# Crossbar transposes issued earlier on the sync queue, first V and pair copies on VectorE, smaller memsets, in a fused attention and maxout-FFN kernel

## The chip, the cores and the metric

The kernel runs on one core of a Trainium2 chip. The metric is device time in microseconds (us) of one execution; a profiled execution gives the trace, whose span is about 1.8 us shorter than that run's time. The granted clock is the share of TensorE's full clock that the profile shows it was given. On one core, a run over 1.5% above the fastest of its kernel is called slow, and ratios leave it out.

## The reference

The input is q, k and v of shape (8 batches, 12 heads, 448 positions, 64), and four 768x768 weights. In float32:

```
scores = q @ k^T / 8
m = max(scores);  e = exp(scores - m)
attn = e / (sum(e) + exp(-m) + 1e-9)          # softmax with one extra "off" slot
x = (attn @ v), heads side by side            # (3584, 768)
h = max(x @ w1, x @ w2, x @ w3)
out = h @ w_out                               # (3584, 768)
```

## The kernel before

Work is cut into 24 groups: 4 heads of one batch each, 3 groups to a batch. A group needs k and q transposed (head dimension on partitions) for the scores, V copied into a buffer with an added column (so that AV also gives the row sums), and its result x transposed again for the FFN. The FFN of a batch is cut into pieces of six matmuls (`p_i` up, `op_ps` out). TensorE's program interleaves the pieces with the scores and AV of later groups, so that it has work while ScalarE does the exponentials.

The first three groups (one batch) run in six half-groups, with k and q transposed by TensorE, as they still are for groups 3 and 4. From group 5 on, the crossbar of the DMA transposes them, issued on the sync queue:

```python
    def pair_qk(i):                       # two heads side by side, fp16; two buffers for each
        qf, kf = raw[i].pop("q"), raw[i].pop("k")
        ...
                nc.gpsimd.tensor_copy(out=t16, in_=f[:, 2 * pr : 2 * pr + 2].rearrange("p h c d -> p c h d"))

    def transpose_dma(i):                 # four crossbar transposes for a group
        ...
                nc.sync.dma_start_transpose(out=t[:, n * S : (n + 1) * S]..., in_=paired[i][pr][n]...)

    def prep_v(i):
        nc.gpsimd.tensor_copy(out=v_buf[i % NE][0:SC, :, :, 0:D], in_=raw[i].pop("v"))

    def x_transpose_dma(i):               # one crossbar transpose: x of a group, after AV and its division
        nc.sync.dma_start_transpose(out=xt_tile(b)..., in_=xn[i]...)
```

Stores of `out` go on the sync queue too; loads are issued by GpSimd. The loop over groups 3 to 23:

```python
    for i in range(3, NI):
        if i + 3 < NI:
            load_group(i + 3)
        if i + 2 < NI:
            pair_qk(i + 2)
        if i > 3:
            prep_v(i)
        ...
        for vi, units in enumerate(visits):           # three visits
            scores(i, units)
            # ... (i == 3 apart) fill with FFN pieces, which issue stores
                if vi < 2:
                    av(i - 1, vi)
                if vi == 1:
                    x_transpose_dma(i - 1)
                    if i + 1 < NI and i + 1 >= PE_QK:   # PE_QK = 5
                        transpose_dma(i + 1)
                fill(per / 6)
```

The waits that the framework adds are all on data and buffers. In the traces each engine's queue, the sync queue too, issues in program order.

The softmax here doesn't subtract the row's maximum and nothing guards it: scores larger than these inputs give would overflow.

Of the kernel before, what the change touches and what calls it, by code (L numbers as in the profile page):

```python
# [2 lines left out]

# [7 lines left out]
FP32 = mybir.dt.float32  # L11
# [10 lines left out]
def kernel(  # L22
# [11 lines left out]
    nc = tc.nc  # L34

    B, H, S, D = q.shape
# [3 lines left out]
    NCH = S // SC  # L40
    NDC = DM // 128
    NFC = DFF // 128
    GH = 4
    NG = H // GH
    NI = B * NG
    HQ = S // 2
# [4 lines left out]
    PE_QK = 5  # L51
# [32 lines left out]
    def load_group(i, which="qkv", step=GH):  # L84
        b, g = groups[i]
        tiles = raw.setdefault(i, {})
        for name in which:
            tiles[name] = ld_pool.tile(
                [SC, GH, NCH, D], MMDT, tag="ld_" + name, name="ld_" + name
            )  # L90
        for h0 in range(0, GH, step):
            for name in which:
                src = {"q": q, "k": k, "v": v}[name][b].rearrange(
                    "(g h) (p c) d -> g p h (c d)", g=NG, c=NCH
                )[g]
                nc.gpsimd.dma_start(  # L96
                    out=tiles[name][:, h0 : h0 + step].rearrange("p h c d -> p h (c d)"),
                    in_=src[:, h0 : h0 + step],
                )
# [22 lines left out]
    EW = NCH * S  # L122
    e_buf = [cpool.tile([128, GH * EW + 16], MMDT, name=f"e{j}") for j in range(NE)]
    v_buf = [cpool.tile([128, GH, NCH, D1], MMDT, name=f"vx{j}") for j in range(NE)]

    def e4(j):
        return e_buf[j][:, 0 : GH * EW].rearrange("p (h c s) -> p h c s", h=GH, c=NCH)

    for j in range(NE):
        nc.vector.memset(v_buf[j][:, :, :, D : D + 2], 1.0 / LAMBDA)  # L130
        nc.vector.memset(v_buf[j][96:128, :, :, 0:D], 0.0)
        nc.vector.memset(e4(j)[:, :, :, HQ : HQ + 16], 0.0)
        nc.vector.memset(e4(j)[96:128, :, 0, :], 1.0)
        nc.vector.memset(e4(j)[96:128, :, 1, 0:16], 0.0)
        nc.vector.memset(e_buf[j][:, GH * EW : GH * EW + 16], 0.0)

    def warm(n, cols=512):
        ps = ps_b.tile([128, 512], FP32, tag="b", name="warm")
# [5 lines left out]
    paired = {}  # L144
    qkT = {}

    def pair_qk(i):
        qf, kf = raw[i].pop("q"), raw[i].pop("k")
        got = []
        for pr in range(GH // 2):  # L150
            t = []
            for nm, f in (("k", kf), ("q", qf)):
                t16 = p16_pool.tile([SC, NCH, 2, D], MMDT, tag=f"{nm}16_{pr}", name=f"{nm}16_{pr}")
                nc.gpsimd.tensor_copy(  # L154
                    out=t16, in_=f[:, 2 * pr : 2 * pr + 2].rearrange("p h c d -> p c h d")
                )
                t.append(t16)
            got.append(t)
        paired[i] = got

    def transpose_pe(i, pr):

        trT = ps_b.tile([128, 2, S], MMDT, tag="b", name="trT")
        for n, nm in enumerate(("k", "q")):
            for c in range(NCH):
                if i in paired:
                    nc.tensor.transpose(
                        out=trT[:, n, ts(c, SC)], in_=paired[i][pr][n][:, c, :, :],
                        identity=ident16[0:SC, 0:SC],
                    )  # L170
                    continue
                for hh in range(2):
                    nc.tensor.transpose(  # L173
                        out=trT[hh * D : hh * D + D, n, ts(c, SC)],
                        in_=raw[i][nm][:, 2 * pr + hh, c, :],
                        identity=ident16[0:SC, 0:SC],
                    )
        t = att_pool.tile([2 * D, 2 * S], MMDT, tag="qkT", name="qkT")
        nc.vector.tensor_copy(out=t, in_=trT.rearrange("p n s -> p (n s)"))  # L179
        qkT[i, pr] = t  # L180

    def transpose_dma(i):
        for pr in range(GH // 2):
            t = att_pool.tile([2 * D, 2 * S], MMDT, tag="qkT", name="qkT")
            for n in range(2):
                nc.sync.dma_start_transpose(  # L186
                    out=t[:, n * S : (n + 1) * S].rearrange("p (c r) -> p c r", c=NCH),
                    in_=paired[i][pr][n].rearrange("p c h d -> p (c h d)"),
                )
            qkT[i, pr] = t  # L190
        paired.pop(i)

    def prep_v(i):
        nc.gpsimd.tensor_copy(  # L194
            out=v_buf[i % NE][0:SC, :, :, 0:D], in_=raw[i].pop("v")
        )

# [63 lines left out]
    def x_transpose_pe(i, qcs):  # L261
        b, g = groups[i]
        nq = len(qcs)
        tp = ps_b.tile([128, 2, nq, SC], MMDT, tag="b", name="xtp")
        for pr in range(2):
            for j, qc in enumerate(qcs):
                nc.tensor.transpose(
                    out=tp[:, pr, j, :],
                    in_=xn[i][:, pr, qc].rearrange("p h d -> p (h d)"),
                    identity=ident16[0:SC, 0:SC],  # L270
                )
        dst = xt_tile(b)[:, 2 * g : 2 * g + 2, qcs[0] * SC : (qcs[0] + nq) * SC]
        nc.vector.tensor_copy(out=dst, in_=tp.rearrange("p a j s -> p a (j s)"))
# [90 lines left out]
    def fill(cols):  # L364
        credit[0] += cols
        while pieces and credit[0] > 0:
            f, a, w = pieces.pop(0)
            f(*a)
            credit[0] -= w
        if not pieces:  # L370
            credit[0] = min(credit[0], 0.0)
# [13 lines left out]
    def half_scores(g, half, n):  # L385
        scores(g, half_units[n : n + 1], half * HQ, HQ)
# [6 lines left out]
    for n, (half, g) in enumerate(halves):  # L393
        for u in range(4):
            half_scores(g, half, u)
            if half == 0 and u in (0, 2) and tpose:
                transpose_pe(*tpose.pop(0))
            if half == 0 and u == 1:
                prep_v(g)
            if n > 0:  # L400
                ph, pg = halves[n - 1]
                if u == 0:
                    av(pg, 0, qh[ph])
                elif u == 2:
                    av(pg, 1, qh[ph])
                elif u == 3:
                    x_transpose_pe(pg, qh[ph])
                    if pg == NG - 1:
                        add_up(0, 0, HQ, [(i, f) for i in range(2) for f in (0, 2, 4)])
            fill(1.2 * UP if half == 1 else 0)  # L410
        if n == 1:
            load_weight(2)
            load_group(3, "v")
            load_group(4)
            load_weight(3)
        if n == 3:
            pair_qk(3)
        if n == 5:
            load_group(5)
            pair_qk(4)  # L420
            transpose_pe(3, 0)
            transpose_pe(3, 1)
            prep_v(3)


    visits = (((0, (0,)), (0, (1,)), (0, (2,))), ((0, (3,)), (1, (0,)), (1, (1,))), ((1, (2,)), (1, (3,))))
    for i in range(3, NI):
        b, g = groups[i]
        if i + 3 < NI:
            load_group(i + 3)  # L430
        if i + 2 < NI:
            pair_qk(i + 2)
        if i > 3:
            prep_v(i)
        if i >= 7 and i % 3 == 1:
            add_batch(i // 3 - 1)
        per = 0.0

        def share():
            nxt = 7 if i < 7 else (i - 1) // 3 * 3 + 4  # L440
            return left() / max(1, nxt - i)

        for vi, units in enumerate(visits):
            scores(i, units)
            if i == 3:
                halfq = qh[1]
                if vi == 0:
                    av(2, 0, halfq)
                    fill(UP)
                    av(2, 1, halfq)  # L450
                    x_transpose_pe(2, halfq)
                    add_up(0, HQ, HQ, [(w, f) for w in range(2) for f in (0, 2, 4)])
                    add_up(0, 0, HQ, [(2, f) for f in (0, 2, 4)])
                    add_up(0, HQ, HQ, [(2, f) for f in (0, 2, 4)])
                    add_out(0)
                    per = share()
                else:
                    if vi == 1:
                        transpose_pe(4, 0)
                        transpose_pe(4, 1)  # L460
                fill(per / 3)
            else:
                if vi == 0:
                    per = share()
                fill(per / 6)
                if vi < 2:
                    av(i - 1, vi)
                if vi == 1:
                    x_transpose_dma(i - 1)
                    if i + 1 < NI and i + 1 >= PE_QK:  # L470
                        transpose_dma(i + 1)
                fill(per / 6)

    av(NI - 1, 0)
    av(NI - 1, 1)
# [34 lines left out]
```

## Time and profile before

| | before |
|---|---|
| median of the first 3 runs | 425.34 us (419.53 to 425.52) |
| span of the profiled run | 421.8 us |
| TensorE busy | 355.0 us |
| mean granted clock | 0.949 |

The page's busy line, and two rows of its picture in 40 slices (busy tenths of TensorE, and its granted clock):

```profile
PE 355.0 (84%) x3438; PEld 203.7 (48%) x3438; DVE 181.5 (43%) x343; ACT 165.0 (39%) x193; POOL 133.4 (32%) x200
PE   5664989676799989799979969879968898899995
PEclk9995999896899999899989998998998999999999
```

TensorE is the engine to feed: it is idle for 67 us of the span, and no other engine is busy for half of the span. What TensorE's matmuls waited for (us in total, times, longest):

```profile
PE stp L207 <- DMA qkT<-q: 38.8, 19, 5.3
PE avp L237 <- POOL vx L194: 11.9, 2, 8.7
PE stp L207 <- DVE qkT L179: 4.9, 3, 4.4
PE avp L237 <- ACT e L216: 2.0, 3, 0.7
```

The first line is one wait for each of groups 5 to 23: the scores stand until the crossbar has brought the transposed q. Why it is late can be seen in one iteration. First the sync queue (`SPq`; start, length, what), then TensorE:

```profile
244.82 1.46 SPq L277 DMA_TRANSPOSE xT<-xn  x1
246.38 1.29 SPq L186 DMA_TRANSPOSE qkT<-k  x1
247.76 1.21 SPq L186 DMA_TRANSPOSE qkT<-q  x1
249.08 2.21 SPq L186 DMA_TRANSPOSE qkT<-k  x1
...
252.68 4.18 SPq L339 DMA_DIRECT2D out_dram<-o_sb  x6
```

```profile
242.61 1.21 PE L237 MATMUL avp<-vx,e 113*128 113x65 f16 x32
...
246.19 3.10 PE L316 MATMUL op_ps<-w,hT 128*128 128x384 f16 x18
253.15 1.30 PE L207 MATMUL stp<-qkT 64*128 64x448 f16 x6 [3.86 <-DMA qkT<-q]
```

x's transpose starts at 244.8, as soon as VectorE's division after the AV at 242.6 is done (244.79). Only then do those of k and q follow. TensorE ran out of other work at 249.3. The six score matmuls after this wait took 1.30 us; after waits of 1.6 us or less they take 0.74. After the long waits the granted clock is lower: it is 0.50 over the three microseconds from 253.15, and 1.00 again from 257.15.

In the start, AV of groups 0 and 2 waited for V copies in GpSimd's queue. TensorE, then GpSimd:

```profile
19.93 1.04 PE L237 MATMUL avp<-vx,e 113*128 113x65 f16 x16 [3.19 <-POOL vx L194]
...
37.62 1.04 PE L237 MATMUL avp<-vx,e 113*128 113x65 f16 x16 [8.73 <-POOL vx L194]
```

```profile
35.81 0.71 POOL L108 DMA_DIRECT2D w<-in_moe_w_out_dram  x1 [1.13 <-DMA w<-in_moe_w_dram]
36.52 1.05 POOL L194 COPY vx<-ld_v 112x1024 f16<-112x1024 f16 x1
```

V of group 2 had landed at 18 us (a GpSimd issue that waited for it was let go then), but its copy stood behind ten load issues, nine of which waited for earlier loads to finish.

### The profile page before, as it was taken

The numbers are of one execution on the slowest core, as the hardware profiler recorded it, in microseconds if no ns is written. First come the engines' busy times: TensorE is split into PE (matmuls) and PEld (weight loads), VectorE is DVE, ScalarE is ACT, GpSimd is POOL, SyncE is SP. The second block draws the span as 40 slices with busy tenths as digits, with TensorE's granted clock in tenths as the row PEclk, the third lists the DMA queues.
The fourth block names the chain that finished last, engine by engine and source line by source line (L and its number), as shares of the span: only waits on it lengthen the run. The fifth ranks groups of instructions, "written<-read, shape, count | busy, mean of one in ns | idle before, by whom it ended". The sixth has DMA issues, their size and how long they took to land.

```text
span 421.8 us, 8277 instructions
## 1 busy us (share of the span) xinstructions
PE 355.0 (84%) x3438; PEld 203.7 (48%) x3438; DVE 181.5 (43%) x343; ACT 165.0 (39%) x193; POOL 133.4 (32%) x200
## 2 busy tenths in 40 slices
PE   5664989676799989799979969879968898899995
PEld 1342757553355545445525435435434465465552
DVE  7241554241254454345435433434432454455553
ACT  1462457543534445345533424444433354440000
POOL 8647445135225324324522414423413130000000
PEclk9995999896899999899989998998998999999999
DMA  8999986376685498587694399385591335313005
GB/s 96 192 207 202 167 105 76 66 78 120 135 143 80 86 153 172 90 120 102 158 129 65 68 164 180 70 127 71 147 133 32 63 75 146 67 23 108 27 2 150
DMA packets 97190, 46.33 MB, mean 110 GB/s; under 512 B 58240, under 2 KB 93568, under 8 KB 97152
## 3 DMA queue, kind: packets, MB, share of 16 engines
q0 software_dynamic: 36704, 21.24, 37.7%
q1 hardware_dynamic: 60448, 24.56, 27.6%
q8 instruction: 27, 0.44, 0.5%
q14 instruction: 11, 0.09, 0.1%
HBM read 42.47 MB, written 11.01 MB: 127 GB/s over the span
## 4 chain that ended last, share of the span: by engine, by line
PE 64%; DMA 21%; SPq 7%; DVE 3%; issue 2%; POOL 1%; ACT 1%; ACTq 0%; POOLq 0%
PE p_i L294 33%; DMA qkT<-q 14%; PE avp L237 12%; PE op_ps L316 9%; PE stp L207 9%; DMA w<-in_moe_w_dram 6%; SPq L186 6%; SPq L277 2%; DMA ld_k<-in_k_dram 1%; DVE hT L305 1%; ACT e L216 1%; DVE xn L249 1%; DVE o_sb L323 1%; POOL ld_k L96 0%; POOL ld_q L96 0%
## 5 line engine op out<-in xcount | busy, mean ns | idle before, releaser
L216 ACT ACTIVATE e<-stp 112x896 f16<-112x896 f32 x192 | 163.7, 916 | 210.4 <-PE stp L207 210.1
L294 PE MATMUL p_i<-xT,w 128*128 128x448 f16 (+1 forms) x972 | 185.0, 341 | 0.6 <-DVE qkT L179 0.3
L294 PEld LDWEIGHTS <-w 128*128 128x128 f16 x972 | 90.6, 100 | 80.4 <-issue 25.5
L305 DVE TENSOR_TENSOR hT<-hT,p_i 128x448 f16<-128x448 f16 x96 | 59.6, 621 | 92.0 <-PE p_i L294 92.0
L207 PE MATMUL stp<-qkT 64*128 64x448 f16 (+1 forms) x432 | 56.4, 360 | 44.4 <-DMA qkT<-q 38.8
L154 POOL COPY k<-ld_k 112x512 f16<-112x512 f16 x42 | 25.9, 618 | 169.1 <-DMA qkT<-k 161.4
L237 PE MATMUL avp<-vx,e 112*128 112x65 f16 (+1 forms) x1536 | 62.1, 198 | 14.2 <-POOL vx L194 11.9
L237 PEld LDWEIGHTS <-e 112*128 112x128 f16 (+1 forms) x1536 | 59.7, 101 | 24.8 <-issue 16.5
L316 PE MATMUL op_ps<-w,hT 128*128 128x384 f16 x336 | 60.0, 330 | 0.0
L303 DVE CAST hT<-p_i 128x448 f16<-128x448 f32 x48 | 30.0, 625 | 52.7 <-PE p_i L294 52.7
L207 PEld LDWEIGHTS <-qkT 64*128 64x128 f16 x432 | 16.6, 98 | 72.9 <-issue 33.6
L323 DVE TENSOR_SCALAR o_sb<-op_ps 128x384 f32<-128x384 f32 x56 | 31.1, 557 | 36.0 <-PE op_ps L316 32.2
L316 PEld LDWEIGHTS <-hT 128*128 128x128 f16 x336 | 31.3, 99 | 24.9 <-issue 5.9
L249 DVE TENSOR_TENSOR xn<-avp,rb 112x512 f16<-112x512 f32 (+1 forms) x54 | 34.1, 632 | 1.9
L154 POOL COPY q<-ld_q 112x512 f16<-112x512 f16 x42 | 26.0, 618 | 21.3 <-DMA qkT<-q 21.3
L246 DVE RECIPROCAL rb<-avp 112x8 f32<-112x8 f32 (+1 forms) x54 | 10.9, 202 | 41.5 <-PE avp L237 41.4
L194 POOL COPY vx<-ld_v 112x1024 f16<-112x1024 f16 x24 | 24.9, 1045 | 7.2 <-PE avp L237 4.6
L96 POOL DMA_DIRECT2D ld_k<-in_k_dram x25 | 17.6, 706 | 2.4 <-DMA w<-in_moe_w_dram 1.1
L96 POOL DMA_DIRECT2D ld_q<-in_q_dram x25 | 17.5, 701 | 0.9 <-DMA ld_k<-in_k_dram 0.5
L96 POOL DMA_DIRECT2D ld_v<-in_v_dram x24 | 16.9, 704 | 1.7 <-DMA w<-in_moe_w_dram 1.2
L179 DVE COPY qkT<-trT 128x896 f16<-128x896 f16 x10 | 6.1, 622 | 6.8 <-PE trT L173 6.2
L108 POOL DMA_DIRECT2D w<-in_moe_w_dram x9 | 6.4, 707 | 4.6 <-DMA w<-in_moe_w_dram 1.9
(28 smaller groups left out, 40.7 us busy)
## 6 DMA issues: line engine op xcount, KB each, us to landing
ld_v<-in_v_dram POOLq DMA_DIRECT2D x24, 224.0 KB, 6.9
ld_k<-in_k_dram POOLq DMA_DIRECT2D x23, 224.0 KB, 6.0
ld_q<-in_q_dram POOLq DMA_DIRECT2D x23, 224.0 KB, 4.2
w<-in_moe_w_dram POOLq DMA_DIRECT2D x9, 384.0 KB, 12.9
out_dram<-o_sb SPq DMA_DIRECT2D x8, 336.0 KB, 3.7
out_dram<-o_sb SPq DMA_DIRECT2D x8, 288.0 KB, 3.3
out_dram<-o_sb SPq DMA_DIRECT2D x8, 240.0 KB, 3.7
out_dram<-o_sb SPq DMA_DIRECT2D x8, 192.0 KB, 3.4
```

The source lines that it names most:

```text
L96: nc.gpsimd.dma_start(out=tiles[name][:, h0 : h0 + step].rearrange("p h c d -> p h (c d)"), in_=src[:, h0 : h0 + step],)
L154: nc.gpsimd.tensor_copy(out=t16, in_=f[:, 2 * pr : 2 * pr + 2].rearrange("p h c d -> p c h d"))
L186: nc.sync.dma_start_transpose(out=t[:, n * S : (n + 1) * S].rearrange("p (c r) -> p c r", c=NCH), in_=paired[i][pr][n].rearrange("p c h d ...
L207: nc.tensor.matmul(out=stp[:, hh, j * qn : (j + 1) * qn], lhsT=t[hh * D : hh * D + D, c * SC : c * SC + 128], rhs=t[hh * D : hh * D + D, S ...
L216: nc.scalar.activation(out=eT[0:SC, 2 * pr : 2 * pr + 2, cs[0] : cs[0] + len(cs), q0 : q0 + qn], in_=stp[0:SC, :, 0 : len(cs) * qn].rearra ...
L237: nc.tensor.matmul(out=ps[:, hh, j * (D + 1) : (j + 1) * (D + 1)], lhsT=eF[0:kk, o : o + 128], rhs=vx[0:kk, h, c, 0 : D + 1], start=(c == ...
L249: nc.vector.tensor_tensor(out=xn[i][:, pr, qcs[0] : qcs[0] + nq].rearrange("p j h d -> p h j d"), in0=acc[:, :, :, 0:D], in1=rb[:, :, 0:nq ...
L294: nc.tensor.matmul(out=p_i[:, j * qn : (j + 1) * qn], lhsT=w_sb[i][:, dc, ts(fc, 128)], rhs=xT[b][:, dc, q0 : q0 + qn], start=(dc == 0), s ...
L303: nc.vector.tensor_copy(out=dst, in_=src)
L305: nc.vector.tensor_tensor(out=dst, in0=dst, in1=src, op=ALU.max)
L316: nc.tensor.matmul(out=op_ps[:, 0:NW], lhsT=hT[bp][:, fc, ts(t, 128)], rhs=wout_sb[:, fc, ts(nh, NW)], start=(fc == 0), stop=(fc == NFC - 1),)
L323: nc.vector.tensor_scalar(out=o_sb[:, ts(nh, NW)], in0=op_ps[:, 0:NW], scalar1=1.0 / LAMBDA, scalar2=None, op0=ALU.mult,)
```

## The change

The intent: issue the k and q transposes of group i+1 at the top of iteration i, before x's transpose and before that iteration's stores; take the early V copies off GpSimd; shorten what VectorE does before its first eviction (its copy of the k and q that TensorE transposed, `qkT<-trT`). The diff, cut to its core:

```diff
+    one2 = struct.unpack("<f", struct.pack("<HH", 0x3C00, 0x3C00))[0]   # two fp16 ones as one fp32
     for j in range(NE):
+        ... (e_buf and v_buf memsets, now with two fp16 values as one fp32 element)
+        nc.vector.memset(ones[:, :, 0, :], one2)
-        nc.vector.memset(e4(j)[96:128, :, 0, :], 1.0)
         ...
-    def pair_qk(i):            # and prep_v(i)
+    def pair_qk(i, eng):       # and prep_v(i, eng)
@@ first batch, half-groups
-                prep_v(g)
+                prep_v(g, nc.vector)
-        if n == 3:
-            pair_qk(3)
         if n == 5:
+            pair_qk(3, nc.vector)
             load_group(5)
-            pair_qk(4)
             transpose_pe(3, 0)
             transpose_pe(3, 1)
-            prep_v(3)
@@ loop
-        if i + 3 < NI:
+        if i + 1 < NI and i + 1 >= PE_QK:
+            transpose_dma(i + 1)
+        if i < 5:
             load_group(i + 3)
         if i + 2 < NI:
-            pair_qk(i + 2)
-        if i > 3:
-            prep_v(i)
+            pair_qk(i + 2, nc.gpsimd)
+        if i > 5:
+            prep_v(i, nc.gpsimd)
+        if 5 <= i < NI - 3:
+            load_group(i + 3)
@@ visits of group 3: pair_qk(4, nc.vector) in the second, its TensorE transposes in the third
@@ visits of the other groups
                     x_transpose_dma(i - 1)
-                    if i + 1 < NI and i + 1 >= PE_QK:
-                        transpose_dma(i + 1)
@@ end of an iteration
+        if i <= 5:
+            prep_v(i, nc.vector)
```

## The prediction

> **What bounds it now.** The span is 421.8 us; TensorE is busy for 355 (busy table). The waits view puts nearly all its other time into three groups: 38.8 us in 19 waits of the scores for the crossbar-transposed q, one per group from 81 us on (longest 5.3); 11.9 us in two waits of AV for V copies on GpSimd (3.2 before 19.9 us, 8.7 before 37.6); 4.4 us for the first qkT eviction. The chain of waits shows the steady cause: AV, its division, transpose of x (1.2 us issue on the sync queue), transposes of k and q (1.3 us issue each), 2.4 to 6.4 us of DMA, then scores.
>
> After waits of 3 us and more, the granted clock is 0.59 to 0.78 over the next 4 to 7 us; six score matmuls took 1.30 us instead of 0.74, twelve up matmuls 3.26 instead of 2.44. The Trainium skill (TensorE: Matmul & The Clock Gate, Part 1) describes this: about 3.4 us of idle halves the clock. The trace agrees.
>
> **What changes.**
> 1. The k and q transposes of group i+1 go to the sync queue at the start of iteration i, ahead of x's, 8 to 10 us earlier. They need 5.2 us of issue plus 2.4 to 6.4 us to land; an iteration's warm TensorE work is 13.3 to 14.5 us (measured between waits), so they should land in time. The pair buffers, for which GpSimd waits 161 us, come free earlier too.
> 2. V copies of groups 0 to 5 move to VectorE, off a GpSimd queue stuck behind weight-load issues. GpSimd's releases show when loads land: V0 13.3 us, V1 16.9, V2 18.1, w1 by 32.0. So the 8.7 us wait goes. Of the 3.2, most: VectorE will now stop for V0 before the next qkT eviction, but group 1's q lands at 12.1 anyway.
> 3. The ones memset at half the elements saves about 0.7 us in each of three rounds; the first scores come 2 us sooner, mostly swallowed, because the next transposes wait for loads.
> 4. Pair copies of groups 3 and 4 on VectorE: estimate 0.2 to 0.3 us each, eight in all (0.62 on GpSimd); about 1 us of new TensorE wait before group 3's transposes.
>
> **Sum.** Start: 3 to 4 us from V0 and evictions, 8.7 from V2, less 1 for VectorE's new copies, perhaps limited by w1: -12 us. Loop: -36 of the 38.8, -8 of cold clock (estimate: eight long waits, 1 to 1.5 us each), +4 for new small waits: -40 us. The tail after 375 us is unchanged. Span about 370 us, time about 372.
>
> **What would show it.** Waits of scores for transposed q below 5 us in total; no AV wait on V above 2 us; idle TensorE 20 to 25 us instead of 67; clock above 0.97; iterations of 13.3 to 14.5 us instead of 15.7; TensorE 85 to 90% of the chain of waits, DMA only in its first 40 us. VectorE's first wait is for V0.
>
> **What would make it wrong.** Transposes of k and q colliding with loads or stores so that they still land late, or x's landing late behind them, stalling the first up matmuls of every third iteration; the start bound by weight loads (205 GB/s from 10 to 50 us) so that the 12 us shrinks to 5; VectorE stopping for a load in front of evictions; a lower granted clock when TensorE no longer pauses. The other way, a warm clock throughout could bring 362.
>
> Chances: faster 0.97, within 2% 0.02, slower 0.01. Predicted 372 us, 8 in 10 between 361 and 388.

## The result and the profile after

| | before | after |
|---|---|---|
| median of 4 runs | 425.43 us (419.53 to 427.64) | 360.26 us (358.55 to 361.95) |
| ratio of the fast runs | | 0.8507 (95%: 0.8407 to 0.8608) |
| span of the profiled run | 421.8 us | 356.8 us |
| TensorE busy | 355.0 us | 339.4 us |
| mean granted clock | 0.949 | 0.986 |

A ratio here is the mean time of one kernel's fast runs over that of the other's of the same rounds, so it is not quite the ratio of the medians quoted. The results are correct in both.

The same lines of the page, for the kernel after:

```profile
PE 339.4 (95%) x3438; PEld 196.2 (55%) x3438; DVE 185.4 (52%) x357; ACT 165.0 (46%) x193; POOL 122.0 (34%) x186
PE   6789789999999999999999999999999999999994
PEclk9599999999999999999999999999999999999999
```

And its longest waits of TensorE's matmuls:

```profile
PE stp L211 <- DVE qkT L183: 3.7, 4, 2.1
PE avp L241 <- ACT e L220: 2.0, 3, 0.7
PE xtp L271 <- DVE xn L253: 1.4, 5, 0.5
```

There is no wait for the crossbar left, and none of AV for V on GpSimd. To see where the 65.0 us of span went, both traces can be cut at two events that both have: the first full-width scores of group 3 (56.28 us before, 43.46 after) and the last AV of the last group (376.73 and 311.75). The stretches are called start, loop and tail from here on. Each line is one stretch: from and to, its length, busy us and instructions of TensorE, of its weight loads, of VectorE, ScalarE and GpSimd, then granted clock, DMA share and GB/s. Before:

```profile
0.00:56.28 56.28, 37.07 (x470) 24.48 (x470) 23.40 (x58) 22.42 (x25) 34.44 (x55) 0.91 1.14 170
56.28:376.73 320.45, 278.09 (x2694) 156.88 (x2695) 134.82 (x246) 142.60 (x168) 99.01 (x146) 0.95 0.63 105
376.73:421.80 45.07, 39.89 (x275) 22.37 (x273) 23.30 (x40) 0.00 (x0) 0.00 (x0) 0.98 0.23 67
```

After:

```profile
0.00:43.46 43.46, 35.16 (x471) 22.89 (x472) 23.52 (x65) 22.64 (x25) 24.56 (x40) 0.88 1.14 174
43.46:311.75 268.29, 264.36 (x2695) 150.94 (x2696) 138.53 (x253) 142.40 (x168) 97.40 (x146) 1.00 0.92 133
311.75:356.80 45.05, 39.89 (x275) 22.36 (x273) 23.31 (x40) 0.00 (x0) 0.00 (x0) 1.00 0.24 67
```

The start got 12.8 us shorter, the loop 52.2 us, and the tail stayed. In the loop TensorE's idle time (length less busy) fell from 42.4 to 3.9 us, which is 38.4 us. Its busy time fell by 13.7 us with the same matmuls, while the clock rose from 0.95 to 1.00. So the loop's gain has two parts, and the smaller is a quarter of it.

How early the transposes now are can be seen on the sync queue. One iteration after, then TensorE at the point that uses them:

```profile
109.12 1.22 SPq L281 DMA_TRANSPOSE xT<-xn  x1
110.44 1.20 SPq L190 DMA_TRANSPOSE qkT<-k  x1
111.74 1.21 SPq L190 DMA_TRANSPOSE qkT<-q  x1
...
118.79 1.17 SPq L343 DMA_DIRECT2D out_dram<-o_sb  x2
```

```profile
126.37 0.74 PE L211 MATMUL stp<-qkT 64*128 64x448 f16 x6
```

The transposes at 110.4 belong to the program's next iteration, which begins on TensorE at 113.2. Behind x's transpose of the iteration before, the queue had nothing more to wait for, so it ran ahead, and they were issued 16 us before the scores at 126.4. In the example of before, the first k transpose was issued 6.8 us ahead of its scores. That slack is used: with more traffic in less time, a k or q transpose took 5.8 us from issue to landing in the median (2.4 before) and 9.8 at worst (7.4 before), and no score waited.

### The profile page after: what moved, and what is told of

The parts are those of the page before. It is cut to its first block, busy times and chain, and to the rows that moved or that the text cites. A ratio compares the mean times of both kernels' runs of the same rounds, so it can differ in the third digit from the quotient of the medians.

```text
span 356.8 us, 8320 instructions
## 1 busy us (share of the span) xinstructions
PE 339.4 (95%) x3438; PEld 196.2 (55%) x3438; DVE 185.4 (52%) x357; ACT 165.0 (46%) x193; POOL 122.0 (34%) x186
## 3 DMA queue, kind: packets, MB, share of 16 engines
q1 hardware_dynamic: 60448, 24.56, 35.9%
## 4 chain that ended last, share of the span: by engine, by line
PE 89%; DVE 3%; ACT 3%; DMA 2%; POOL 1%; issue 1%; ACTq 0%; POOLq 0%
PE p_i L298 47%; PE op_ps L320 15%; PE avp L241 14%; PE stp L211 11%; ACT e L220 3%; DMA ld_v<-in_v_dram 2%; DVE xn L253 1%; PE trT L177 1%; POOL ld_k L97 1%; POOL ld_q L97 1%; DVE q L158 0%; DVE k L158 0%; DVE xT L277 0%; DVE qkT L183 0%; DVE hT L307 0%
## 5 line engine op out<-in xcount | busy, mean ns | idle before, releaser
L298 PE MATMUL p_i<-xT,w 128*128 128x448 f16 (+1 forms) x972 | 178.1, 332 | 0.3
L298 PEld LDWEIGHTS <-w 128*128 128x128 f16 x972 | 88.6, 98 | 74.6 <-issue 17.8
L158 POOL COPY k<-ld_k 112x512 f16<-112x512 f16 x38 | 23.5, 619 | 127.1 <-DMA qkT<-k 69.7
L241 PEld LDWEIGHTS <-e 112*128 112x128 f16 (+1 forms) x1536 | 56.8, 99 | 11.5 <-issue 3.1
L241 PE MATMUL avp<-vx,e 112*128 112x65 f16 (+1 forms) x1536 | 59.5, 195 | 2.3 <-ACT e L220 2.0
L320 PE MATMUL op_ps<-w,hT 128*128 128x384 f16 x336 | 59.0, 326 | 0.0
L211 PE MATMUL stp<-qkT 64*128 64x448 f16 (+1 forms) x432 | 52.7, 339 | 4.7 <-DVE qkT L183 3.7
L211 PEld LDWEIGHTS <-qkT 64*128 64x128 f16 x432 | 14.7, 95 | 33.1 <-issue 21.5
L158 POOL COPY q<-ld_q 112x512 f16<-112x512 f16 x38 | 23.6, 622 | 3.5 <-DMA qkT<-q 3.4
L198 POOL COPY vx<-ld_v 112x1024 f16<-112x1024 f16 x18 | 18.7, 1044 | 9.5 <-issue 9.5
```

Source lines behind the costliest of these rows:

```text
L158: eng.tensor_copy(out=t16, in_=f[:, 2 * pr : 2 * pr + 2].rearrange("p h c d -> p c h d"))
L198: eng.tensor_copy(out=v_buf[i % NE][0:SC, :, :, 0:D], in_=raw[i].pop("v"))
L211: nc.tensor.matmul(out=stp[:, hh, j * qn : (j + 1) * qn], lhsT=t[hh * D : hh * D + D, c * SC : c * SC + 128], rhs=t[hh * D : hh * D + D, S ...
L241: nc.tensor.matmul(out=ps[:, hh, j * (D + 1) : (j + 1) * (D + 1)], lhsT=eF[0:kk, o : o + 128], rhs=vx[0:kk, h, c, 0 : D + 1], start=(c == ...
L298: nc.tensor.matmul(out=p_i[:, j * qn : (j + 1) * qn], lhsT=w_sb[i][:, dc, ts(fc, 128)], rhs=xT[b][:, dc, q0 : q0 + qn], start=(dc == 0), s ...
L320: nc.tensor.matmul(out=op_ps[:, 0:NW], lhsT=hT[bp][:, fc, ts(t, 128)], rhs=wout_sb[:, fc, ts(nh, NW)], start=(fc == 0), stop=(fc == NFC - 1),)
```

## The experiments

Twelve kernels ran, all with correct results. They came in three sets of four, each set on one chip and beside runs of the kernel before there. For set 1, the kernel before took 421.77 us (median of 7), for set 2 424.25 (of 11), for set 3 423.43 (of 11). The runs of before scatter by up to 2.8% on one chip, so that in sets 2 and 3 many (6 and 8 of 11) count as slow and the ratios there rest on the remaining 5 and 3. In set 2 variants are compared with c1 by the means of their fast runs.

The lengths of start and loop in each profile, cut at the same two events; the tail was 45.0 to 45.1 us in all:

| run | median us | start | loop |
|---|---|---|---|
| before | 425.43 | 56.3 | 320.5 |
| after | 360.26 | 43.5 | 268.3 |
| e1_order_only | 374.11 | 56.7 | 274.5 |
| e2_all_but_order | 408.39 | 44.6 | 317.4 |
| e3_swap_in_place | 365.91 | 42.4 | 276.9 |
| e4_v_only | 410.87 | 44.8 | 318.0 |
| c1_after_again | 359.85 | 43.2 | 273.5 |
| e5_old_memsets | 360.43 | 44.1 | 269.4 |
| e6_pairs_gpsimd | 359.14 | 41.6 | 270.9 |
| e9_start | 363.49 | 42.6 | 272.7 |
| e7_p16_3 | 415.68 | 56.3 | 314.2 |
| e8_warm | 414.16 | 58.1 | 310.1 |
| e10_loads_first | 360.05 | 42.2 | 268.4 |
| e11_v3_early | 358.22 | 41.2 | 270.3 |

### e1_order_only: only the order on the sync queue

```diff
 # kernel before
     for i in range(3, NI):
         b, g = groups[i]
+        if i + 1 < NI and i + 1 >= PE_QK:
+            transpose_dma(i + 1)
 ...
                     x_transpose_dma(i - 1)
-                    if i + 1 < NI and i + 1 >= PE_QK:
-                        transpose_dma(i + 1)
```

> The kernel before with one edit: the transposes of group i+1 are issued at the top of iteration i; everything else as before (V and pair copies on GpSimd, old memsets). Theory (the sync queue works in order, so before, the k and q transposes stood behind x's transpose, which waits for AV and its division): the whole loop gain of 52.7 us and nothing of the start, 370 to 378 us, no wait of the scores for transposed q after the first two groups, the two V waits of 3.2 and 8.7 us still there. Rival (the gain comes from GpSimd being relieved of V copies, so that pairs are ready earlier): 405 us or more.

Measured: 374.11 us, ratio 0.8849 (0.8789 to 0.8909). The profiled run was a slow one (377.97 us), so its lines are read for what waits and not for its length. Its waits of TensorE:

```profile
PE avp L237 <- POOL vx L194: 10.3, 2, 7.8
PE stp L207 <- DVE qkT L179: 5.2, 3, 4.8
PE p_i L294 <- DMA xT<-xn: 4.8, 2, 3.2
```

The wait of the scores for the crossbar is gone and the V waits are still there, as the theory said. The third line is the price: x's transpose now stands behind those of k and q, and twice in this run the first up matmuls of a batch had to wait for it.

### e2_all_but_order: everything except the order

```diff
 # kernel after
-        if i + 1 < NI and i + 1 >= PE_QK:
-            transpose_dma(i + 1)
 ...
                     x_transpose_dma(i - 1)
+                    if i + 1 < NI and i + 1 >= PE_QK:
+                        transpose_dma(i + 1)
```

> The changed kernel with the transposes put back behind x's transpose. Theory: only the start's 12 to 13 us are left, 408 to 418 us, waits of the scores for transposed q again 33 to 44 us in total, granted clock about 0.95. Rival (GpSimd relief): below 385 us.

Measured: 408.39 us, ratio 0.9676 (0.9633 to 0.9719). The wait is back:

```profile
PE stp L211 <- DMA qkT<-q: 37.9, 19, 3.8
```

With e1 this settles the loop: by the profiles, the order alone takes 46.0 us of the 52.2 off it (in e1's slow run), and everything else in the change only 3.0. By medians of that set, e1 saves 47.7 us and e2 13.4; the sum, 61.0, is near the 64 to 65 of the whole change on other chips. Relieving GpSimd of V copies is refuted as the cause of the loop's gain.

### e3_swap_in_place: ahead of x, but not ahead of the stores

```diff
 # kernel after, the lines at the top of the iteration taken out
                 if vi == 1:
+                    if i + 1 < NI and i + 1 >= PE_QK:
+                        transpose_dma(i + 1)
                     x_transpose_dma(i - 1)
```

> The changed kernel with the k and q transposes where they were before in the program (behind the stores of the iteration's first part), but ahead of x's transpose. Theory: the queue is held up mainly by x's wait for AV, so most of the gain stays, 362 to 376 us; what is lost is in the iterations with stores, where x's transpose is now issued up to 5 us late and the first up matmuls of each batch wait about 2 us for it. Rival (being ahead of the stores is what counts): 385 us or more, with the waits of the scores for q back in the two iterations of three that have stores.

Measured: 365.91 us, ratio 0.8678 (0.8642 to 0.8714). An iteration with stores, on the sync queue:

```profile
121.48 1.17 SPq L343 DMA_DIRECT2D out_dram<-o_sb  x2
122.76 1.23 SPq L190 DMA_TRANSPOSE qkT<-k  x1
...
127.99 1.25 SPq L281 DMA_TRANSPOSE xT<-xn  x1
```

and what TensorE then did at the start of the next batch:

```profile
132.23 0.54 PE L298 MATMUL p_i<-xT,w 128*128 128x448 f16 x2 [1.56 <-DMA xT<-xn]
```

Getting ahead of x is worth most of it: behind x, the transposes of k and q wait for the AV of the same iteration; ahead of it, only for that of the iteration before. What getting ahead of the stores adds is less sure. It is 1.6 to 2% by the ratios (0.8678 against 0.8541 and 0.8507 for the changed kernel), but these come from other chips, and e10, nearly the changed kernel, has a ratio of 0.8646 on a third. The mechanism can be seen in the profile: here the transposes waited for the stores and pushed x's back, and the up matmuls waited for x three times (4.4 us), the scores once for q (2.6 us).

### e4_v_only: only the V copies of groups 0 to 5 on VectorE

```diff
 # kernel before: prep_v(i) becomes prep_v(i, eng)
-                prep_v(g)
+                prep_v(g, nc.vector)
 # and prep_v(3, nc.vector); in the loop:
-            prep_v(i)
+            prep_v(i, nc.vector if i <= 5 else nc.gpsimd)
```

> The kernel before with one edit: the V copies of groups 0 to 5 on VectorE. Theory: both AV waits on V go (3.2 and 8.7 us) and the cold clock behind them, 409 to 415 us, the loop's waits for transposed q unchanged near 39 us. Rival (the start is bound by the weight loads at 205 GB/s, so that an earlier AV only waits for w1): 419 us or more, with a new wait of the up matmuls for w in the first 40 us.

Measured: 410.87 us, ratio 0.9719 (0.9662 to 0.9777). Its start is 44.8 us, against 56.3 before and 43.5 after: the V copies are worth 11.5 of the 12.8 us there. The waits of AV for V are gone, and no wait for w appeared. The loop still waited 35.9 us for q.

### e5_old_memsets: the memsets of before in the changed kernel

The edit is the memset block of the kernel before in place of the new one.

> The changed kernel with the memsets as before. Theory (the first evictions come 2 us later, but the second group's q lands only at 12 us and V of group 0 at 13 us, so the delay is swallowed): 0 to 0.7 us longer than the changed kernel. Rival (the memsets sit at the head of the chain of the start, every microsecond counts): 2 us or more longer.

Measured beside c1 (below): mean of the fast runs 360.6 us against 360.1. The first scores came at 10.91 us instead of 8.20, but the start became only 0.6 us longer, and no difference of the times is shown. The new memset took 0.81 us where the old took 1.55; that saving is off the critical path, as expected.

### c1_after_again: the changed kernel as the yardstick of set 2

> The changed kernel again, as the yardstick of this chip for the three runs beside it: 358 to 362 us.

Measured: 359.85 us, ratio 0.8541 (0.8484 to 0.8599). Its profiled run, at 363.45 us, was among its longer ones, and shows one thing that varies from run to run:

```profile
PE p_i L298 <- DMA xT<-xn: 3.2, 3, 2.7
```

In that execution x's transpose was late at batch starts; in the profile shown above it never was. These 3.2 us are part of the 5.2 by which its loop is longer.

### e6_pairs_gpsimd: pair copies of groups 3 and 4 back on GpSimd

```diff
 # kernel after
+        if n == 3:
+            pair_qk(3, nc.gpsimd)
         if n == 5:
-            pair_qk(3, nc.vector)
             load_group(5)
+            pair_qk(4, nc.gpsimd)
 ...
-                    if vi == 1:
-                        pair_qk(4, nc.vector)
-                    else:
+                    if vi == 1:
                         transpose_pe(4, 0)
```

> The changed kernel with the pair copies of groups 3 and 4 back on GpSimd. Theory: these copies on VectorE cost TensorE three waits (0.69, 0.32 and 0.60 us) in front of the transposes of groups 3 and 4; back on GpSimd, these go, 0 to 1.5 us shorter than the changed kernel. Rival (GpSimd's queue is late behind the weight-load issues there, so the copies would come late): 1 us or more longer, with a TensorE wait for the pair copies on GpSimd.

Measured: 359.14 us; mean of the fast runs 359.4, against 360.1 of c1. The three waits in front of the transposes of groups 3 and 4 went, and the start became about 2 us shorter. Then 2.1 us were given back to a new wait, of AV for the V copy of group 3. That copy on VectorE, and what GpSimd did meanwhile:

```profile
54.67 2.18 DVE L198 COPY vx<-ld_v 112x1024 f16<-112x1024 f16 x1
```

```profile
54.84 0.62 POOL L158 COPY k<-ld_k 112x512 f16<-112x512 f16 x1
55.40 0.62 POOL L158 COPY q<-ld_q 112x512 f16<-112x512 f16 x1
55.95 0.61 POOL L158 COPY k<-ld_k 112x512 f16<-112x512 f16 x1
56.51 0.81 POOL L158 COPY q<-ld_q 112x512 f16<-112x512 f16 x1
```

The same copy with GpSimd between its own took 0.42 us in the kernel after (at 57.03). The Trainium skill (GPSIMD Engine Reference, 1. Specifications) says that GpSimd's SBUF interfaces are shared with VectorE, with contention with VectorE instructions in a 2-port mode. The trace agrees in that the copy ended only when GpSimd's row of four was nearly through; it does not show in which mode the copy ran.

### e9_start: a version meant to be better

```diff
 # kernel after
-            if half == 0 and u == 1:
+            if half == 0 and u == 2:
                 prep_v(g, nc.vector)
 ...
+        if n == 4:
+            pair_qk(3, nc.vector)
         if n == 5:
-            pair_qk(3, nc.vector)
 ...
     transpose_pe(0, 0)
+    warm(8)                      # eight matmuls on zeros
```

> A version meant to be better: the changed kernel with the V copies of groups 0 to 2 one eviction later in VectorE's order, the pair copies of group 3 one half-group earlier, and eight filler matmuls on zeros in the 2 us wait before the first scores, to keep the clock up. Theory: VectorE no longer stops for V of group 0 before an eviction (about 0.9 us), the wait before group 3's transposes goes (about 1 us) and the clock stays at full rate from 9 to 19 us (up to 2 us): 2 to 4 us shorter than the changed kernel. If the start is bound by loads all the same: within 0.5 us of it.

Measured: 363.49 us, 0.8% longer than c1 by the means of the fast runs (363.1 against 360.1). The theory fell. The start did become 0.9 us shorter than in the kernel after, less than hoped; an up piece now came before w1 had landed and waited 0.8 us for it. But the loop was 4.4 us longer than in the profile of after shown above:

```profile
PE p_i L298 <- DMA xT<-xn: 3.5, 3, 1.9
...
PE avp L241 <- DVE vx L198: 1.5, 1, 1.5
```

The second line is the contention of e6 again: TensorE's earlier arrival put VectorE's V copy beside GpSimd's pair copies, and it took 1.59 us. The first is x landing late at three batch starts. Why that should come with an earlier start is not shown: c1 has the same waits in one profile without this edit.

### e7_p16_3: three buffers for the pairs in the kernel before

```diff
-    p16_pool = ctx.enter_context(tc.tile_pool(name="p16", bufs=2))
+    p16_pool = ctx.enter_context(tc.tile_pool(name="p16", bufs=3))
```

> The kernel before with three buffers for the fp16 pairs instead of two. Rival (GpSimd waited 161 us for these buffers, so they were the bottleneck, and freeing them early is what helped): the waits of the scores for transposed q shrink by 15 us or more, 405 us or less. Theory (those waits of GpSimd were off the critical path, the pairs were ready long before x's transpose let the queue go on): GpSimd's wait for the buffers moves elsewhere, the scores still wait 33 to 44 us, time within 1% of the kernel before.

Measured: 415.68 us, ratio 0.9965 (0.9862 to 1.0068): unclear, with no difference shown. (By medians it is 1.8% shorter, but 8 of the 11 runs of before in this set count as slow.) The page's wait line that looked alarming before, GpSimd's 161.4 us for pair buffers, became 148.6, and the scores' wait did not move much:

```profile
PE stp L207 <- DMA qkT<-q: 35.4, 19, 4.4
```

So the longest line of a list of waits belonged to an engine whose waiting cost little. GpSimd's wait for the buffers did not move elsewhere, as was expected, and the sync queue's own short waits for the pairs hardly changed (13.9 us in 22 waits before, 12.9 in 20 here), so a third buffer brought the pairs little earlier. That late pairs were not the bottleneck is seen more directly in those waits of before: none was longer than 1.2 us, while the queue stood 143.9 us in 20 waits ahead of the transposes of x (the first, at the start, left out).

### e8_warm: useless matmuls inside the waits of the kernel before

```diff
+        if i in (5, 6, 7, 11, 14, 16, 20):
+            warm(12)
         for vi, units in enumerate(visits):
             scores(i, units)
```

> The kernel before with twelve filler matmuls on zeros (about 2.6 us at full clock) ahead of the scores of groups 5, 6, 7, 11, 14, 16 and 20, where the trace of before shows waits of 2.2 to 5.3 us. 84 matmuls of useless work. Theory (these waits also cost a halved clock afterwards, 13.9 us in all over the loop): the fillers sit inside waits that were there anyway, the clock stays up, 8 to 13 us shorter than the kernel before. Rival (the extra busy time before is only an artefact of how ends of matmuls are modelled, the clock costs nothing): same time or up to 4 us longer.

Measured: 414.16 us against 423.43 by medians of all runs, but ratio 0.9917 (0.9828 to 1.0006) by the fast ones: whether the kernel got faster is unclear. The trace is clearer about the mechanism. A filled wait, and the loop of this run:

```profile
95.08 2.75 PE L140 MATMUL warm<-wz 128*128 128x512 f16 x12
99.13 0.74 PE L207 MATMUL stp<-qkT 64*128 64x448 f16 x6 [1.30 <-DMA qkT<-q]
```

```profile
58.13:368.22 310.09, 284.96 (x2779) 161.19 (x2780) 134.64 (x246) 142.60 (x168) 98.78 (x146) 0.99 0.68 109
```

The wait of group 6 is still some 4 us in all (fillers and rest), but the scores after it take 0.74 us, not 1.30. In the loop the clock is 0.99 instead of 0.95. The waits themselves did not shrink: the remaining waits for q are 20.6 us, which with the fillers (below) makes 38.7, against 38.8 before. Twelve fillers take about 2.6 us (11 steps fill 2.75 less the 0.38 of the last one, so 0.216 each), seven lots 18.1 us; without them TensorE's own work took 266.8 us, against 278.1 before with the same matmuls, and 264.4 after. So most (11.3) of the 13.7 us of busy time that the change saved in the loop was the clock, which stayed up when TensorE did not pause. This profile's loop is 10.4 us shorter than before's, while its start is 1.9 us longer at a clock of 0.74.

### e10_loads_first: the loads of group i+3 at the top of the iteration again

```diff
-        if i < 5:
-            load_group(i + 3)
+        if i + 3 < NI:
+            load_group(i + 3)
 ...
-        if 5 <= i < NI - 3:
-            load_group(i + 3)
```

> The changed kernel with the loads of group i+3 issued at the top of every iteration, ahead of the pair and V copies, as before. Theory (GpSimd runs ahead either way, transposes land in 2.3 to 9.8 us and have an iteration of 13.3 us to do so): within 1% of the changed kernel, 357 to 364 us. Rival (the later loads are what keeps the transposes' transfers free of collisions): 366 us or more, with waits of the scores for transposed q of 5 us or more.

Measured: 360.05 us, ratio 0.8646 (0.8557 to 0.8735); by median the same as the changed kernel, which ran on another chip. In its profile no score waits for q. Moving the loads did nothing that can be seen.

### e11_v3_early: e6, and V of group 3 copied earlier

```diff
 # e6
             transpose_pe(3, 1)
+            prep_v(3, nc.vector)
 ...
-        if i <= 5:
+        if 4 <= i <= 5:
             prep_v(i, nc.vector)
```

> A version meant to be better: the changed kernel with the pair copies of groups 3 and 4 on GpSimd (as in the run with that edit alone, in whose trace VectorE's copy of V of group 3 took 2.18 us instead of 0.42 beside four GpSimd copies, and AV waited 2.1 us for it) and V of group 3 copied one stage earlier. Theory (the 2.1 us wait was for the copy alone): AV no longer waits for V, 355 to 358.5 us. If x's transposes are late in some iterations, as they were for 3.2 us in one profile of the changed kernel, up to 361.

Measured: 358.22 us (357.63 to 360.79), ratio 0.86 (0.854 to 0.8659). The wait of AV for V is gone and its start, 41.2 us, is the shortest of all. Its median is the lowest by 2 us against the changed kernel's 360.26, but they ran on different chips, the ratios do not separate them, and a lead of half a per cent is not shown.

## Why the prediction was right or wrong

**Direction and size of the whole: right, with the gain too small.** It said 372 us, a saving of 53, and 361 to 388. The saving was 65. The median, 360.26 us, is just below the range's lower end, though the ratio 0.8507 of the stated 425.34 us is 361.8, just inside.

**The signs: right in direction, two of them further than foreseen.** Clock 0.986 (above 0.97), TensorE 89% of the chain of waits (85 to 90), no wait for transposed q (below 5 us). Idle TensorE time, 17.4 us, lies below the 20 to 25 foreseen, and the iteration from 113.18 to 126.37, 13.2 us, just below 13.3 to 14.5.

**Step 1, the order on the sync queue: right.** e1 and e2 show it from both sides. e2 refutes one rival (GpSimd's load); against the other (pair buffers) speak e7, weakly, and the sync queue's short waits for pairs in before (there). The prediction had the transposes issued 8 to 10 us earlier. In the two examples above the lead over the scores grew from 6.8 to 15.9 us, so by 9.1. Over groups 8 to 23 it is 11 to 17 us after, the smaller leads behind six stores, and 3.7 to 7.9 before.

**Step 2, V copies: right.** e4 gives 11.5 us for them in the start. As predicted, VectorE's first wait for data from a load was for V of group 0, 3.2 us, and it stood before an eviction. (The weight loads of the start move 199 GB/s from 10 to 50 us in the trace, not 205.)

**Step 3, memsets: right.** Swallowed by the loads (e5).

**Step 4, pair copies on VectorE: right in part.** Three of the eight took 0.27 to 0.28 us, as estimated; a fourth took 0.52, and those of group 4, which ran beside GpSimd's copies, 0.57 to 0.70. TensorE got three new waits of 0.3 to 0.7 us, 1.6 in all instead of about 1 (e6 removes them).

**The sum: where it was short.** The start was foreseen at -12 and came at -12.8. The step that was off is "Loop: -36 of the 38.8, -8 of cold clock (estimate: eight long waits, 1 to 1.5 us each), +4 for new small waits: -40 us". The measured terms are -38.4 for idle time, all old waits and new ones together, and -13.7 for busy time, together -52.2. So 5.7 us of the 12 were the cold clock. The count of eight was right: in the loop of before, the granted clock fell to 0.50 at just eight waits, five of 3.0 to 5.3 us and three of 2.2 to 2.6, and in the loop of after at none. What was mis-sized is the cost of each: taken microsecond by microsecond over the 8 us behind each wait, the clock that was missing adds up to 1.5 to 2.6 us, 13.9 in all and 1.7 in the mean, where 1 to 1.5 was estimated and 1 put into the sum. The other 6.4 us are the wait terms: -36 and +4 were set where -38.4 came. The new waits that the +4 stood for do exist, but they come and go: none in the profile of after, 3.2 us in that of c1.

**What would make it wrong.** Of the dangers named, "x's landing late behind them" is real, at 4.4 us in e3, 3.2 in c1 and 3.5 in e9. "A lower granted clock when TensorE no longer pauses" was not seen: the loop's clock is 1.00. A danger that was not named is that VectorE's fast copies become slow beside GpSimd's.

## What to carry to other kernels

An in-order DMA queue should carry first what can go first: one transfer that waits for a late result holds up everything behind it, and moving ready transfers ahead let the queue here run 11 to 17 us ahead, about an iteration. When a wait of the bottleneck engine goes, count its clock as well as its idle time: here the clock was a quarter of the loop's gain. Once TensorE is busy without a gap, small improvements elsewhere need a run, not a sum: in the profiles of e6 and e9 the start was 1.9 and 0.9 us shorter than in that of after, and the loop 2.6 and 4.4 us longer, in part through a new collision.

## What the Trainium skill lacked or had wrong

- TensorE: Matmul & The Clock Gate, Part 1, gives at least one idle window of about 3.4 us, one that runs free, as what turns the clock down. In the kernel before, a wait of 2.20 us (before 283.66 us) was followed by scores at 1.30 us, as slow as after the longest waits, and by a granted clock of 0.50 for three microseconds. A longer wait need not do so: in e2, after one of 3.60 us (before 210.25 us), the clock stayed at 1.00. And the fall can come late: in e7, after 3.33 us (before 187.32 us), the scores still took 0.74, but the six up matmuls behind them 2.42 instead of 1.31. A window of idle as long as 3.4 us was not needed, and the length of a wait did not decide it alone.
- GPSIMD Engine Reference, 1. Specifications, names the contention with VectorE but gives no size for it there (the page SBUF — State Buffer treats it at more length; its account was not compared with these traces). Here a 112x1024 fp16 copy on VectorE grew from 0.42 to 2.18 us beside four GpSimd copies, and 112x512 ones from 0.28 to between 0.57 and 0.70, while the GpSimd copies took 0.61 to 0.81 (0.62 in the mean in the kernel before).
- VectorE: DVE Perf Modes, "Zero memsets can be issued as uint32 (trn2)", speaks of zeros only. The same halving works for a constant whose pair of fp16 values is one fp32: 1792 fp16 ones took 1.55 us, 896 fp32 elements with the same bytes 0.81.
